# Last inverse DFT stage on quarter tiles of the array, and gated sums clamped at -1 in place of a Relu pass

## The chip, the core and the metric

One core of a Trainium2 chip runs the whole kernel as one program. The metric is the device time of one execution in microseconds, the median of several runs. What the trace shows is one further execution, with a profiler on.

## The reference

The input `x` is 8 x 3072 x 256 in float32. Along the 3072 positions each batch is transformed, mixed with a complex 256 x 256 weight, shrunk towards zero and transformed back; then a two-layer network with a gate runs over all 24576 rows.

```python
X = np.fft.rfft(x, axis=1)
Yr = Xr @ w_r - Xi @ w_i + b_r
Yi = Xr @ w_i + Xi @ w_r + b_i
Yr = np.sign(Yr) * np.maximum(np.abs(Yr) - lam, 0.0)     # lam = 0.01, the same for Yi
y = np.fft.irfft(Y, n=x.shape[1], axis=1)
h = y.reshape(B * S, D) @ w_in                           # 256 -> 2048
g = np.where(h >= 1, h, np.where(h <= -1, 0.0, (h + 1) ** 2 / 4))
out = g @ w_out                                          # 2048 -> 256
```

## The kernel before

The transform of length 3072 = 48 x 64 is done by matmuls. The first part of the program (up to about 566 us) runs a loop over 96 units `u` (8 batches x 12 pairs of frequency groups): `stage1` and `stage2` are the forward transform, `mix` multiplies with the complex weights, `shrink` shrinks, `stage3` is the first half of the inverse transform and stores its result to DRAM (`u_d`).

The last inverse stage is `stage4`. Its unit is a block `c` of four positions: `load_u(c)` brings 96 rows x 4 positions x 256 channels from `u_d` to `uin`; 64 blocks cover everything. For each half of 128 channels (`d`) and each position (`jj`) one float32 matmul takes 96 rows x 128 channels of `uin` as the stationary operand and the 96 x 96 table `c2_sb` as the moving one. In the trace every float32 matmul stands as two passes, each with a weight load (LDWEIGHTS on the row PEld) and a MATMUL: 8 matmuls of a block are 16 of each. `stage4_out` copies a half-block of results (128 x 384) from PSUM to `yt`, on ScalarE. The table `c2` couples a row 2g+c, which holds one of two parities `h`, only with columns of the same parity, so half of its entries are zero.

The second part is the network, a loop over 384 units `n`: 48 tiles of 512 rows, each with 8 pairs of 128 hidden columns. Each pair is formed by seven products of half-size blocks (Strassen's scheme in Winograd's form, `product`, three matmuls each, since every factor is split in a high and a low part), in PSUM tiles `ps_yz` (tag C) and `ps_xv` (tag D). `snap` copies a partial sum to SBUF (ScalarE), `sum_first` and `sum_second` add on VectorE to give `h`; then `ramp` (Relu of 0.5 h + 0.5) and `square` on ScalarE, `gate` on VectorE (max with 1, min with the square), `split_hi` (ScalarE) and `split_lo` (VectorE), and three units later `down` multiplies with `w_out` into the accumulators `accA` and `accB`, in eight pieces `D_(0..7)` that stand between the products. The program is written out by hand in this order; each engine runs its own instructions in the order in which they are issued, and waits on semaphores for the others.

`stage4` of the first two half-batches (8 blocks) lies in the last units of the first part and in units 0 and 1 of the second (`quarter4`, `leftover`). The other 56 blocks lie one each at the end of 56 of the 384 units of the second part, behind `D_(4, 5, 6, 7)` (`if n in four`), in two buffers of tag D.

Of the kernel before, what the change touches and what calls it, by code (L numbers as in the profile page):

```python
# [8 lines left out]

F32 = mybir.dt.float32  # L10
# [11 lines left out]
LAM = 0.01  # L22


def dft_constants(S):
# [55 lines left out]
    return np.stack([hi, round_r(a - hi.astype(np.float64))])  # L81


def constants(S):
    c1, c2, t, ti = dft_constants(S)
    return {
        "c1": np.ascontiguousarray(parts(c1).transpose(1, 0, 2)),
        "c2": c2.astype(np.float32),
        "t": np.ascontiguousarray(t.transpose(1, 0, 2).astype(np.float32)),
        "ti": np.ascontiguousarray(ti.transpose(1, 0, 2).astype(np.float32)),  # L90
    }
# [3 lines left out]
def tile_fft_mix_moe(  # L95
    ctx: ExitStack, tc: tile.TileContext, x, w_r, w_i, b_r, b_i, w_in, w_out, c1, c2, t_f, t_i, out
):
    nc = tc.nc
    B, S, D = x.shape
    DFF = w_in.shape[1]  # L100
    NF = DFF // P
    ND = D // P
    JT = 4
# [12 lines left out]
    NUNIT = NT * NP  # L116

    left = lambda name, **k: tc.alloc_tile_pool(name=name, bufs=1, side="left", reuse_waits="tile", **k)
# [15 lines left out]
    ug = [a.rearrange("(g p) j d -> (p j) g d", g=G) for a in u_d]  # L134


    win = [[keep.tile([P, 7, P], F32R, name=f"win{k}{p}") for p in range(NP)] for k in "hl"]
    wout = keep.tile([P, NF, 2, D], F32R, name="wout")
    c2_sb = keep.tile([Q, Q], F32, name="c2_sb")
    half = keep.tile([P, 1], F32, name="half")  # L140

    c1_sb = first_st.tile([Q, 2, Q], F32R, name="c1_sb")
# [4 lines left out]
    bias = fold.tile([P, D], F32, name="bias")  # L147
# [255 lines left out]
    def stage4(c, d, into=None):  # L403
        hb, m = divmod(c, JH // JT)
        a = uin[c] if d < ND - 1 else uin.pop(c)
        if m == 0 and d == 0:
            yt[hb] = pools["in"].tile([P, ND, Q, JH], F32, tag="yt", bufs=2, name="yt")
        if into is None:
            bufs_D = 2 if "ff" in pools else 3
            ps = pools["ps"].tile([P, JT, Q], F32, tag="D", bufs=bufs_D, name="ps_i2")  # L410
        else:
            ps = into.rearrange("p k d -> p (k d)")[:, : JT * Q].rearrange("p (j q) -> p j q", j=JT)
        ps4[c, d] = ps
        for jj in range(JT):
            nc.tensor.matmul(ps[:, jj, :], lhsT=a[:, jj, d * P : (d + 1) * P], rhs=c2_sb, start=True, stop=True)  # L415
        if d == ND - 1 and c + 3 < NHB * JH // JT:
            load_u(c + 3)

    def stage4_out(c, d, copy=nc.scalar.copy):
        hb, m = divmod(c, JH // JT)  # L420
        copy(yt[hb][:, d, :, m * JT : (m + 1) * JT], ps4.pop((c, d)).rearrange("p j q -> p q j"))

    ops, raw_t = {}, {}

# [36 lines left out]
    ups, snaps, hs, rs, gs, acc, outs = {}, {}, {}, {}, {}, {}, {}  # L463
# [5 lines left out]
    def product(n, which, to, start):  # L469

        i, p = divmod(n, NP)
        if n not in ups:
            ups[n] = [
                pools["ps"].tile([P, 2, TH], F32, tag="C", bufs=2, name="ps_yz"),
                pools["ps"].tile([P, 2, TH], F32, tag="D", bufs=2, name="ps_xv"),
            ]
        ps = ups[n]["YZXV".index(to) // 2][:, "YZXV".index(to) % 2, :]
        w, m = FACTORS[which - 1]
        hi, lo = ops[i]
        for k, (a, mv) in enumerate(((0, hi), (0, lo), (1, hi))):  # L480
            nc.tensor.matmul(  # L481
                ps, lhsT=win[a][p][:, w, :], rhs=mv[:, m, :], start=start and k == 0, stop=k == 2, skip_group_check=True
            )


    def snap(n, at):
        if n not in snaps:
            snaps[n] = pools["ff"].tile([P, 3, TH], F32, tag="snap", bufs=2, name="snap")
        nc.scalar.copy(snaps[n][:, at, :], ups[n][1][:, 0, :])  # L489


    def sum_second(n):
        h = hs[n] = pools["ff"].tile([P, 4, TH], F32, tag="h", bufs=3, name="h")
        yz, xv = ups[n]
        for to, a in ((2, yz[:, 0, :]), (3, xv[:, 1, :])):
            nc.vector.tensor_tensor(out=h[:, to, :], in0=a, in1=snaps[n][:, 2, :], op=ALU.add)

    def sum_first(n):
        yz, xv = ups.pop(n)
        nc.vector.tensor_tensor(out=hs[n][:, 0:2, :], in0=yz, in1=snaps.pop(n)[:, 0:2, :], op=ALU.add)  # L500

    ALL = slice(0, 4)

    def ramp(n, part=ALL):
        if n not in rs:
            rs[n] = pools["ff"].tile([P, 4, TH], F32, tag="r", bufs=2, name="r")
        nc.scalar.activation(rs[n][:, part], hs[n][:, part], AF.Relu, bias=half, scale=0.5)  # L507

    def square(n, part=ALL):
        nc.scalar.activation(rs[n][:, part], rs[n][:, part], AF.Square)  # L510

    def gate(n, part=ALL):
        h, r = hs[n][:, part], rs[n][:, part]
# [11 lines left out]
    def down(n, piece):  # L525
        if n < 0 or n >= NUNIT:
            return
# [63 lines left out]
    with tc.manual_schedule():  # L591
# [21 lines left out]
        for h in range(FIRST):  # L613
            last = xs[h][0]
# [37 lines left out]
            next(ws, None)  # L652

        stored = FIRST
        four = iter([(c, d) for c in range(2 * JH // JT) for d in range(ND)])

        def quarter4():
            c, d = next(four)
            stage4(c, d)
            stage4_out(c, d)  # L660

        U4 = UN - 6

# [3 lines left out]
        for u in range(UN + 3):  # L667
# [51 lines left out]
            if 1 <= u < UN + 1:  # L719
                shrink(u - 1, more_weights if WU <= u < 84 else lambda: None)  # L720
            if U4 <= u < U4 + 4:
                quarter4()
                quarter4()
            if u == U4 + 4:
                prep_sums(0)
            if u == UN:
                mixing.release()
                pools["ops"] = right("ops")
                prep_split_hi(0, 0)
                prep_split_hi(0, 1)  # L730
                prep_split_lo(0, 0)
                quarter4()
            if u == UN + 1:
                quarter4()
                quarter4()
            if 2 <= u < UN + 2:
                stage3(u - 2)
            if u == UN + 1:
                prep_split_hi(0, 2)
                quarter4()  # L740
                prep_split_lo(0, 1)
                prep_split_lo(0, 2)
        fold.release()
# [3 lines left out]

        LAG = 3
        spare = [pools["ps"].tile([P, 2, 2, D], F32, tag=k, bufs=1, name=f"spare{k}") for k in "AB"]
        rest = [(c, d, spare[k // 2][:, k % 2]) for k, (c, d) in enumerate(four)]  # L750
        four = {}

        def leftover(n):
            if n < NP and rest:
                c, d, into = rest.pop(0)
                stage4(c, d, into)
                stage4_out(c, d, nc.vector.tensor_copy)

        for hb in range(2, NHB):
            for m, at in enumerate((0, 7, 11, 16)):  # L760
# [2 lines left out]
        for n in range(NUNIT + LAG + 1):  # L763
            i, p = divmod(n, NP)
            live = n < NUNIT
            split_step = p - 4 if live and i + 1 < NT and 4 <= p < 7 else None
            n1 = n - 1 if 0 <= n - 1 < NUNIT else None
            n2 = n - 2 if 0 <= n - 2 < NUNIT - 1 else None
            last = n1 == NUNIT - 1
# [9 lines left out]
            if live:  # L779
                product(n, 1, "X", True)  # L780
                snap(n, 1)
                if n == 0:
                    leftover(n)
                product(n, 5, "Y", True)
                if n == 0:
                    leftover(n)
                product(n, 2, "Z", False)
            if out_b is not None:
                output_copy(out_b, 1)
# [7 lines left out]
            if n1 is not None:  # L797
                product(n1, 3, "Y", False)
                sum_first(n1)
            if n == 1:  # L800
                leftover(n)
            if live:
                product(n, 6, "X", False)
                snap(n, 0)
# [7 lines left out]
                output_copy(out_a, 0)  # L812
                output_add(out_a, 0)
            if n1 is not None and not last:
                ramp(n1)
            if last:
                for part in (slice(2, 4), slice(0, 2)):
                    ramp(n1, part)
                    square(n1, part)
                    gate(n1, part)  # L820
                    split_hi(n1, part)
                    split_lo(n1, part)
            if live:
                product(n, 4, "V", False)
                if n == 0:
                    leftover(n)
# [40 lines left out]
```

## Time and profile before

| what | value |
|---|---|
| median of 3 runs | 2732.16 us (2730.28 to 2732.48) |
| the profiled execution | 2729.93 us |
| its span, first to last instruction | 2728.1 us |
| mean granted clock of TensorE | 0.998 of full speed |
| PE busy, share of the span | 2703.3 us, 99% |
| VectorE busy | 2106.2 us, 77% |
| ScalarE busy | 2068.1 us, 76% |
| GpSimd busy | 379.2 us, 14% |

PE stands for TensorE's matmuls, PEld for its weight loads, which overlap the matmuls; DVE is VectorE, ACT is ScalarE, POOL is GpSimd. The span is 1.8 us shorter than the time of its execution. PE's busy time counts every matmul's modelled duration, so two that overlap in the pipeline cover the same time once, and a share of 99% says that PE is nearly never without one, not that it works at its peak.

### The profile page before, as it was taken

The numbers are of one execution on the slowest core, as the hardware profiler recorded it, in microseconds if no ns is written. First come the engines' busy times: TensorE is split into PE (matmuls) and PEld (weight loads), VectorE is DVE, ScalarE is ACT, GpSimd is POOL, SyncE is SP. The second block draws the span as 40 slices with busy tenths as digits, with TensorE's granted clock in tenths as the row PEclk, the third lists the DMA queues.
The fourth block names the chain that finished last, engine by engine and source line by source line (L and its number), as shares of the span: only waits on it lengthen the run. The fifth ranks groups of instructions, "written<-read, shape, count | busy, mean of one in ns | idle before, by whom it ended". The sixth has DMA issues, their size and how long they took to land.

```text
span 2728.1 us, 48377 instructions
## 1 busy us (share of the span) xinstructions
PE 2703.3 (99%) x19296; PEld 2520.5 (92%) x19296; DVE 2106.2 (77%) x2987; ACT 2068.1 (76%) x3458; POOL 379.2 (14%) x372
## 2 busy tenths in 40 slices
PE   8999999999999999999999999999999999999998
PEld 5999999989999999999999999999999999999997
DVE  5899988668777777777777777777777777777786
ACT  5677777567777777787877777777777777777786
POOL 1255433010101010101010010101010101010100
PEclk9999999999999999999999999999999999999999
DMA  8766666410000001000000000000001010100000
GB/s 252 229 215 215 213 215 198 140 58 16 20 28 20 28 20 28 20 28 20 28 20 28 23 25 24 24 28 21 28 20 30 18 34 14 34 14 22 9 17 16
DMA packets 123548, 166.57 MB, mean 61 GB/s; under 512 B 10842, under 2 KB 88506, under 8 KB 123322
## 3 DMA queue, kind: packets, MB, share of 16 engines
q1 hardware_dynamic: 123074, 163.26, 19.8%
q8 instruction: 152, 2.49, 0.4%
q14 instruction: 74, 0.61, 0.1%
q10 hardware_dynamic: 248, 0.20, 0.0%
HBM read 87.93 MB, written 75.50 MB: 60 GB/s over the span
## 4 chain that ended last, share of the span: by engine, by line
PE 95%; DVE 2%; ACT 2%; DMA 1%; issue 0%; SPq 0%; ACTq 0%
PE ps_xv L481 20%; PE ps_yz L481 15%; PE accB L537 13%; PE accA L537 13%; PE ps_mix L260 9%; PE accB L540 7%; PE accA L540 7%; PE ps_i L415 4%; PE ps_f L192 3%; PE ps_f L213 3%; PE ps_i L297 2%; DVE yl L288 0%; DVE xl L180 0%; ACT xh L175 0%; DVE Xl L230 0%
## 5 line engine op out<-in xcount | busy, mean ns | idle before, releaser
L489 ACT COPY snap<-ps_xv 128x256 f32<-128x256 f32 x1152 | 425.6, 369 | 415.4 <-PE ps_xv L481 415.4
L523 DVE TENSOR_TENSOR gl<-h,gh 128x1024 fp32r<-128x1024 f32 x385 | 470.4, 1222 | 258.2 <-ACT gh L519 251.8
L537 PE MATMUL accA<-wout,gh 128*128 128x512 f32 x1536 | 574.3, 396 | 0.6 <-ACT gh L519 0.6
L537 PE MATMUL accB<-wout,gh 128*128 128x512 f32 x1536 | 558.0, 396 | 0.0
L514 DVE SCALAR_TENSOR_TENSOR h<-h,r 128x1024 f32<-128x1024 f32 x385 | 475.3, 1235 | 78.4 <-ACT r L510 78.3
L507 ACT ACTIVATE r<-h,half 128x1024 f32<-128x1024 f32 x385 | 443.8, 1153 | 0.0
L481 PE MATMUL ps_xv<-oph,winh 128*128 128x256 f32 x1536 | 437.6, 285 | 1.7 <-ACT snap L489 1.4
L481 PE MATMUL ps_xv<-opl,winh 128*128 128x256 f32 x1536 | 437.2, 285 | 0.0
L481 PE MATMUL ps_xv<-oph,winl 128*128 128x256 f32 x1536 | 432.0, 281 | 0.0
L540 PE MATMUL accB<-wout,gl 128*128 128x256 f32 x1536 | 429.7, 280 | 0.0
L540 PE MATMUL accA<-wout,gl 128*128 128x256 f32 x1536 | 428.7, 279 | 1.0 <-DVE gl L523 1.0
L510 ACT ACTIVATE r<-r 128x1024 f32<-128x1024 f32 x385 | 410.2, 1066 | 0.1
L519 ACT CAST gh<-h 128x1024 fp32r<-128x1024 f32 x385 | 404.6, 1051 | 2.9 <-DVE h L514 2.9
L500 DVE TENSOR_TENSOR h<-ps_yz,snap 128x512 f32<-128x512 f32 x384 | 265.2, 691 | 132.9 <-PE ps_yz L481 106.5
L436 POOL TENSOR_TENSOR tsum<-yt 128x256 f32<-128x256 f32 x96 | 100.6, 1062 | 1916.4 <-DVE opl L457 1098.6
L537 PEld LDWEIGHTS accB<-wout,gh 128*128 128x128 f32 x1536 | 288.0, 188 | 52.7
L481 PE MATMUL ps_yz<-oph,winl 128*128 128x256 f32 x1152 | 325.4, 282 | 0.0
L481 PE MATMUL ps_yz<-opl,winh 128*128 128x256 f32 x1152 | 324.8, 282 | 0.0
L481 PE MATMUL ps_yz<-oph,winh 128*128 128x256 f32 x1152 | 322.0, 280 | 0.1
L537 PEld LDWEIGHTS accA<-wout,gh 128*128 128x128 f32 x1536 | 288.0, 188 | 36.3 <-ACT gh L519 0.9
L481 PEld LDWEIGHTS ps_xv<-oph,winh 128*128 128x128 f32 x1536 | 288.2, 188 | 34.7 <-ACT snap L489 2.7
L481 PEld LDWEIGHTS ps_xv<-oph,winl 128*128 128x128 f32 x1536 | 292.3, 190 | 0.0
(114 smaller groups left out, 5437.5 us busy)
## 6 DMA issues: line engine op xcount, KB each, us to landing
xin<-in_x SPq DMA_DIRECT2D x128, 192.0 KB
z_d<-zst SPq DMA_DIRECT2D x128, 192.0 KB
zin<-z_d SPq DMA_DIRECT2D x96, 256.0 KB
u_d<-ust SPq DMA_DIRECT2D x96, 256.0 KB
uin<-u_d SPq DMA_DIRECT2D x64, 384.0 KB
out<-ot SPq DMA_DIRECT2D x191, 128.0 KB
wraw<-in_moe_w_in SPq DMA_DIRECT2D x16, 256.0 KB
wraw<-in_moe_w_out SPq DMA_DIRECT2D x16, 256.0 KB
```

The costliest lines, as they stand in the source:

```text
L260: nc.tensor.matmul(ps[:, gi, :], lhsT=a, rhs=wm[nm, k][:, d, :], start=n == 0, stop=n == 6 * ND - 1)
L415: nc.tensor.matmul(ps[:, jj, :], lhsT=a[:, jj, d * P : (d + 1) * P], rhs=c2_sb, start=True, stop=True)
L481: nc.tensor.matmul(ps, lhsT=win[a][p][:, w, :], rhs=mv[:, m, :], start=start and k == 0, stop=k == 2, skip_group_check=True)
L489: nc.scalar.copy(snaps[n][:, at, :], ups[n][1][:, 0, :])
L500: nc.vector.tensor_tensor(out=hs[n][:, 0:2, :], in0=yz, in1=snaps.pop(n)[:, 0:2, :], op=ALU.add)
L507: nc.scalar.activation(rs[n][:, part], hs[n][:, part], AF.Relu, bias=half, scale=0.5)
L510: nc.scalar.activation(rs[n][:, part], rs[n][:, part], AF.Square)
L514: nc.vector.scalar_tensor_tensor(out=h, in0=h, scalar=1.0, in1=r, op0=ALU.max, op1=ALU.min)
L519: nc.scalar.copy(gs[n][0][:, part], hs[n][:, part])
L523: nc.vector.tensor_tensor(out=gl, in0=hs[n][:, part], in1=gh.bitcast(F32), op=ALU.subtract)
L537: nc.tensor.matmul(o, lhsT=gh[:, blk, at : at + P], rhs=wout[:, f], start=f == 0, stop=False, skip_group_check=True)
L540: nc.tensor.matmul(o[:, 0, :], lhsT=gl[:, blk, at : at + P], rhs=wout[:, f, 0, :], start=False, stop=f == NF - 1, skip_group_check=True,)
```

## The change

Three things are changed together.

`stage4` uses the array in quarters. The 96 rows of a block are stored in two sets of 48 rows, one per parity, at partitions 0 and 64 (`load_u` issues two DMAs per block, each of half the bytes), and `c2_sb` holds the 48 x 48 table of either parity, without the zero entries. For each position and each half of 128 channels there are now four float32 matmuls, each with 48 rows x 64 channels as the stationary operand and 48 columns of moving data, on the four 64 x 64 quarters of the array (`tile_position`), in the order (row set, channel half) = (0,0), (1,1), (0,1), (1,0). Both halves `d` of a block are done in one call; each row set writes a PSUM bank of its own, and two copies of 384 elements, one for each bank, take the result to `yt`.

In the second part `stage4` stands ahead of `sum_second` and `D_(4, 5, 6, 7)` in its unit instead of at its end, and its two banks are one of tag D and the C bank that is not the unit's own (C is now two tags, C0 and C1, used in turn).

The sums `h` are clamped from below at -1 as they are formed (`add_floor`, a custom VectorE operation that adds and limits), so that (0.5 h + 0.5) is never negative; the Relu pass `ramp` is gone, and `square` reads `h` with scale and bias itself, at the place at which `ramp` stood.

```diff
-        uin[c] = pools["in"].tile([Q, JT, D], F32, tag="uin", bufs=3, name="uin")
+        uin[c] = pools["in"].tile([P, JT, D], F32, tag="uin", bufs=3, name="uin")
         j = half_b * JH + m * JT
-        nc.sync.dma_start(uin[c], u_d[b][:, j : j + JT, :])
+        for h in range(2):
+            nc.sync.dma_start(uin[c][h * HP : h * HP + R1], uh[b][h, :, j : j + JT, :])
...
         for jj in range(JT):
-            nc.tensor.matmul(ps[:, jj, :], lhsT=a[:, jj, d * P : (d + 1) * P], rhs=c2_sb, start=True, stop=True)
+            for d in range(ND):
+                for h, e in QUARTERS:
+                    rows, cols = slice(h * HP, h * HP + R1), slice(e * HP, (e + 1) * HP)
+                    nc.tensor.matmul(
+                        ps[h][cols, d, jj, :],
+                        lhsT=a[rows, jj, d * P + e * HP : d * P + (e + 1) * HP],
+                        rhs=c2_sb[rows],
+                        start=True,
+                        stop=True,
+                        tile_position=(h * HP, e * HP),
+                    )
...
+    def add_floor(out, a, b):
+        nc.vector._custom_dve(TENSOR_ADD_SAT, out=out, in0=a, in1=b, s0=FLT_MAX, s1=-1.0)
...
-    def ramp(n, part=ALL):
+    def square(n, part=ALL):
         if n not in rs:
             rs[n] = pools["ff"].tile([P, 4, TH], F32, tag="r", bufs=2, name="r")
-        nc.scalar.activation(rs[n][:, part], hs[n][:, part], AF.Relu, bias=half, scale=0.5)
-
-    def square(n, part=ALL):
-        nc.scalar.activation(rs[n][:, part], rs[n][:, part], AF.Square)
+        nc.scalar.activation(rs[n][:, part], hs[n][:, part], AF.Square, bias=half, scale=0.5)
...
                 product(n, 7, "X", False)
                 snap(n, 2)
+                if n in four:
+                    stage4(four[n], [bank("D", 2), bank(f"C{(n + 1) % 2}")])
+                    stage4_out(four[n], [nc.scalar.copy] * 2)
                 sum_second(n)
-            if n1 is not None and not last:
-                square(n1)
             D_(4, 5, 6, 7)
...
-            if n in four:
-                for d in range(ND):
-                    stage4(four[n], d)
-                    stage4_out(four[n], d)
```

On PE, at the end of a unit of the second part with a block, the rows before were these (`accB<-wout` is a piece of `down`, `ps_i` is `stage4`, `ps_xv` with `winh` and `oph` a product of the next unit; the semaphores of an engine carry its name):

```order
L537 MATMUL accB<-wout,gh 128x512
L540 MATMUL accB<-wout,gl 128x256
L415 MATMUL ps_i_24909<-c_sb,uin 128x96 [waits DMAHW4_49,DVE_49]
L415 MATMUL ps_i_24909<-c_sb,uin 128x96 x3
L415 MATMUL ps_i_24915<-c_sb,uin 128x96 [waits DVE_49,Activation_49]
L415 MATMUL ps_i_24915<-c_sb,uin 128x96 x3
```

In the changed kernel the block begins directly behind the unit's last product, and the first rows of its 32 are these, which go on by turns between the two banks:

```order
L505 MATMUL ps_xv<-oph,winh_91 128x256
L505 MATMUL ps_xv<-opl,winh_91 128x256
L505 MATMUL ps_xv<-oph,winl_99 128x256
L429 MATMUL ps_i_25574<-c_sb,uin 64x48 [waits DMAHW1_49,DVE_49]
L429 MATMUL ps_i_25575<-c_sb,uin 64x48 [waits DMAHW2_49,DVE_49]
```

So 8 matmuls of 128 x 96 behind the pieces of `down` have become 32 of 64 x 48 ahead of them.

On ACT the same kind of unit had these rows before (`gh` is `split_hi`, `r<-h` is `ramp`, `r<-r` is `square`, `yt` is `stage4_out`):

```order
L519 CAST gh<-h 128x1024 [waits DVE_49]
L507 ACTIVATE r<-h,half 128x1024 [waits DVE_49]
L489 COPY snap<-ps_xv 128x256 [waits PE_49]
L510 ACTIVATE r<-r 128x1024 [waits Activation_49]
L421 COPY yt<-ps_i_11571 128x96x4 [waits PE_49]
L421 COPY yt<-ps_i_11577 128x96x4 [waits PE_49]
```

Now there is one pass over `h` instead of two:

```order
L543 CAST gh<-h 128x1024 [waits DVE_49]
L534 ACTIVATE r<-h,half 128x1024 [waits DVE_49]
L513 COPY snap<-ps_xv 128x256 [waits PE_49]
L444 COPY yt<-ps_i_11849 128x96x4 [waits PE_49]
L444 COPY yt<-ps_i_11850 128x96x4 [waits PE_49]
```

The row `r<-r` is gone, and the two copies of the block follow the snap directly.

## Rows read from the trace of the kernel before

**Rows 1.** The page's head: span, busy time and share of each engine.

```profile
span 2728.1 us, 48377 instructions
PE 2703.3 (99%) x19296; PEld 2520.5 (92%) x19296; DVE 2106.2 (77%) x2987; ACT 2068.1 (76%) x3458; POOL 379.2 (14%) x372
```

**Rows 2.** The page's chain that ended last, shares by line.

```profile
PE ps_xv L481 20%; PE ps_yz L481 15%; PE accB L537 13%; PE accA L537 13%; PE ps_mix L260 9%; PE accB L540 7%; PE accA L540 7%; PE ps_i L415 4%; PE ps_f L192 3%; PE ps_f L213 3%; PE ps_i L297 2%; DVE yl L288 0%; DVE xl L180 0%; ACT xh L175 0%; DVE Xl L230 0%
```

**Rows 3.** Windows, from:to, length, then each engine's busy time (instructions), clock, DMA.

```profile
566.00:590.00 24.00, 21.19 (x153) 18.82 (x152) 14.25 (x22) 14.43 (x25) 2.83 (x4) 1.00 0.29 78
...
650.00:1200.00 550.00, 550.00 (x3884) 514.40 (x3883) 419.65 (x550) 430.92 (x681) 50.69 (x49) 1.00 0.08 24
```

**Rows 4.** The chain in order of time: start us, us, what.

```profile
519.94 0.72 PE ps_i L297 x6
...
524.43 0.72 PE ps_i L297 x6
525.15 0.89 PE ps_f L213 x8
...
530.67 0.75 PE ps_i L297 x6
...
692.95 0.72 PE ps_xv L481 x6
698.27 0.72 PE ps_xv L481 x6
...
705.38 0.72 PE ps_xv L481 x6
```

**Rows 5.** Timeline of PE and PEld at one block: start us, us, what.

```profile
700.12 1.87 PEld L415 LDWEIGHTS ps_i<-c_sb,uin 96*128 96x128 f32 x16
700.23 1.92 PE L415 MATMUL ps_i<-c_sb,uin 96*128 96x96 f32 x16
...
701.91 0.19 PEld L481 LDWEIGHTS ps_xv<-oph,winh 128*128 128x128 f32 x1
701.94 0.36 PE L481 MATMUL ps_xv<-oph,winh 128*128 128x256 f32 x1
702.02 0.19 PEld L481 LDWEIGHTS ps_xv<-opl,winh 128*128 128x128 f32 x1
```

**Rows 6.** Weight loads by form: count, busy us, mean ns, idle us before.

```profile
L415 PEld LDWEIGHTS ps_i<-c_sb,uin 96*128 96x128 f32 x992 | 116.2, 192 | 2.6
...
L192 PEld LDWEIGHTS ps_f<-xh,c_sb 96*96 96x96 f32 x208 | 30.4, 163 | 3.4
```

**Rows 7.** ACT's groups by form in the second part.

```profile
L507 ACT ACTIVATE r<-h,half 128x1024 f32<-128x1024 f32 x383 | 442.3, 1155 | 0.0
...
L489 ACT COPY snap<-ps_xv 128x256 f32<-128x256 f32 x1152 | 425.6, 369 | 415.4 <-PE ps_xv L481 415.4
L510 ACT ACTIVATE r<-r 128x1024 f32<-128x1024 f32 x383 | 409.0, 1068 | 0.0
L519 ACT CAST gh<-h 128x1024 fp32r<-128x1024 f32 x383 | 403.3, 1053 | 1.3 <-DVE h L514 1.3
...
L421 ACT COPY yt<-ps_i 128x384 f32<-128x384 f32 x124 | 59.5, 480 | 58.5 <-PE ps_i L415 58.5
```

**Rows 8.** DVE's groups by form in the second part.

```profile
L514 DVE SCALAR_TENSOR_TENSOR h<-h,r 128x1024 f32<-128x1024 f32 x383 | 474.0, 1237 | 77.7 <-ACT r L510 77.7
L523 DVE TENSOR_TENSOR gl<-h,gh 128x1024 fp32r<-128x1024 f32 x383 | 469.0, 1225 | 256.8 <-ACT gh L519 250.3
...
L500 DVE TENSOR_TENSOR h<-ps_yz,snap 128x512 f32<-128x512 f32 x384 | 265.2, 691 | 132.9 <-PE ps_yz L481 106.5
...
L496 DVE TENSOR_TENSOR h<-ps_yz,snap 128x256 f32<-128x256 f32 x384 | 163.1, 425 | 30.1 <-ACT snap L489 1.9
```

**Rows 9.** The chain in order of time at the program's end.

```profile
2713.17 0.63 ACT r L507
...
2715.88 0.63 ACT r L507
```

More of the change, by code (lines that the diff above doesn't have):

```diff
@@ L8 @@
 from concourse._compat import with_exitstack
+from concourse.dve_ops import TENSOR_ADD_SAT
 F32 = mybir.dt.float32
@@ L22 @@
 LAM = 0.01
+FLT_MAX = float(np.finfo(np.float32).max)
 def dft_constants(S):
@@ L81, in parts, with two_rows @@
     return np.stack([hi, round_r(a - hi.astype(np.float64))])
+def two_rows(a):
+    o = np.zeros((P, a.shape[1]), a.dtype)
+    for h in range(2):
+        o[h * P // 2 : h * P // 2 + len(a)] = a
+    return o
 def constants(S):
@@ L87, in constants @@
         "c1": np.ascontiguousarray(parts(c1).transpose(1, 0, 2)),
-        "c2": c2.astype(np.float32),
+        "c2": two_rows(c2.reshape(R1, 2, R1, 2)[:, 0, :, 0].astype(np.float32)),
         "t": np.ascontiguousarray(t.transpose(1, 0, 2).astype(np.float32)),
@@ L116, in tile_fft_mix_moe @@
     NUNIT = NT * NP
+    HP = P // 2
+    QUARTERS = ((0, 0), (1, 1), (0, 1), (1, 0))
     left = lambda name, **k: tc.alloc_tile_pool(name=name, bufs=1, side="left", reuse_waits="tile", **k)
@@ L134, in tile_fft_mix_moe @@
     ug = [a.rearrange("(g p) j d -> (p j) g d", g=G) for a in u_d]
+    uh = [a.rearrange("(r h) j d -> h r j d", h=2) for a in u_d]
     win = [[keep.tile([P, 7, P], F32R, name=f"win{k}{p}") for p in range(NP)] for k in "hl"]
     wout = keep.tile([P, NF, 2, D], F32R, name="wout")
-    c2_sb = keep.tile([Q, Q], F32, name="c2_sb")
+    c2_sb = keep.tile([P, R1], F32, name="c2_sb")
     half = keep.tile([P, 1], F32, name="half")
@@ L398, in load_u, with stage4 @@
         b, half_b = divmod(hb, 2)
-        uin[c] = pools["in"].tile([Q, JT, D], F32, tag="uin", bufs=3, name="uin")
+        uin[c] = pools["in"].tile([P, JT, D], F32, tag="uin", bufs=3, name="uin")
         j = half_b * JH + m * JT
-        nc.sync.dma_start(uin[c], u_d[b][:, j : j + JT, :])
-    def stage4(c, d, into=None):
+        for h in range(2):
+            nc.sync.dma_start(uin[c][h * HP : h * HP + R1], uh[b][h, :, j : j + JT, :])
+    def stage4(c, banks):
         hb, m = divmod(c, JH // JT)
-        a = uin[c] if d < ND - 1 else uin.pop(c)
-        if m == 0 and d == 0:
+        a = uin.pop(c)
+        if m == 0:
@@ L416, in stage4 @@
-        if d == ND - 1 and c + 3 < NHB * JH // JT:
+        ps = ps4[c] = [
+            x.rearrange("p a n -> p (a n)")[:, : ND * JT * R1].rearrange("p (d j r) -> p d j r", d=ND, j=JT)
+            for x in banks
+        ]
+        for jj in range(JT):
+            for d in range(ND):
[9 more added lines that the diff above has]
+                    )
@@ L417, in stage4, with stage4_out @@
+        if c + 3 < NHB * JH // JT:
             load_u(c + 3)
-    def stage4_out(c, d, copy=nc.scalar.copy):
+    def stage4_out(c, copies):
         hb, m = divmod(c, JH // JT)
-        copy(yt[hb][:, d, :, m * JT : (m + 1) * JT], ps4.pop((c, d)).rearrange("p j q -> p q j"))
+        to = yt[hb][:, :, :, m * JT : (m + 1) * JT].rearrange("p d (r h) j -> p d r h j", h=2)
+        for h, (copy, ps) in enumerate(zip(copies, ps4.pop(c), strict=True)):
+            copy(to[:, :, :, h, :], ps.rearrange("p d j r -> p d r j"))
@@ L425, in tile_fft_mix_moe, with bank @@
+    def bank(tag, bufs=1):
+        return pools["ps"].tile([P, 2, TH], F32, tag=tag, bufs=bufs, name="ps_i2")
     ops, raw_t = {}, {}
@@ L473, in product @@
             ups[n] = [
-                pools["ps"].tile([P, 2, TH], F32, tag="C", bufs=2, name="ps_yz"),
+                pools["ps"].tile([P, 2, TH], F32, tag=f"C{n % 2}", bufs=1, name="ps_yz"),
                 pools["ps"].tile([P, 2, TH], F32, tag="D", bufs=2, name="ps_xv"),
@@ L495, in sum_second @@
         for to, a in ((2, yz[:, 0, :]), (3, xv[:, 1, :])):
-            nc.vector.tensor_tensor(out=h[:, to, :], in0=a, in1=snaps[n][:, 2, :], op=ALU.add)
+            add_floor(h[:, to, :], a, snaps[n][:, 2, :])
     def sum_first(n):
         yz, xv = ups.pop(n)
-        nc.vector.tensor_tensor(out=hs[n][:, 0:2, :], in0=yz, in1=snaps.pop(n)[:, 0:2, :], op=ALU.add)
+        add_floor(hs[n][:, 0:2, :], yz, snaps.pop(n)[:, 0:2, :])
     ALL = slice(0, 4)
-    def ramp(n, part=ALL):
+    def square(n, part=ALL):
         if n not in rs:
             rs[n] = pools["ff"].tile([P, 4, TH], F32, tag="r", bufs=2, name="r")
-        nc.scalar.activation(rs[n][:, part], hs[n][:, part], AF.Relu, bias=half, scale=0.5)
-    def square(n, part=ALL):
-        nc.scalar.activation(rs[n][:, part], rs[n][:, part], AF.Square)
+        nc.scalar.activation(rs[n][:, part], hs[n][:, part], AF.Square, bias=half, scale=0.5)
     def gate(n, part=ALL):
@@ L654, in tile_fft_mix_moe, with half4 @@
         stored = FIRST
[L655 to L660, printed above, removed]
+        four = iter(range(2 * JH // JT))
+        def half4():
+            c = next(four)
+            stage4(c, [bank(k) for k in "AB"])
+            stage4_out(c, [nc.scalar.copy] * 2)
         U4 = UN - 6
@@ L721, in tile_fft_mix_moe @@
             if U4 <= u < U4 + 4:
-                quarter4()
-                quarter4()
+                half4()
             if u == U4 + 4:
@@ L731, in tile_fft_mix_moe @@
                 prep_split_lo(0, 0)
-                quarter4()
+                half4()
             if u == UN + 1:
-                quarter4()
-                quarter4()
+                half4()
             if 2 <= u < UN + 2:
@@ L749, in tile_fft_mix_moe, with leftover @@
         spare = [pools["ps"].tile([P, 2, 2, D], F32, tag=k, bufs=1, name=f"spare{k}") for k in "AB"]
-        rest = [(c, d, spare[k // 2][:, k % 2]) for k, (c, d) in enumerate(four)]
+        rest = [(c, [x[:, k] for k in range(2)]) for c, x in zip(four, spare, strict=True)]
         four = {}
[L753 to L757, printed above, removed]
+        def leftover():
+            c, banks = rest.pop(0)
+            stage4(c, banks)
+            stage4_out(c, [nc.vector.tensor_copy] * 2)
         for hb in range(2, NHB):
@@ L781, in tile_fft_mix_moe @@
                 snap(n, 1)
-                if n == 0:
-                    leftover(n)
                 product(n, 5, "Y", True)
                 if n == 0:
-                    leftover(n)
+                    leftover()
                 product(n, 2, "Z", False)
@@ L814, in tile_fft_mix_moe @@
             if n1 is not None and not last:
-                ramp(n1)
+                square(n1)
             if last:
                 for part in (slice(2, 4), slice(0, 2)):
-                    ramp(n1, part)
                     square(n1, part)
```

11 lines of the change are left out of this document (1 added, 10 removed).

## The prediction

> **What bounds the kernel now.** I read the page's head first: PE is busy for 2703.3 us of 2728.1, VectorE and ScalarE for about three quarters [rows 1]. The chain that ended last is PE nearly all the way, and `stage4` (L415) has 4% of it [rows 2]. Busy PE can hide waits, so I then took windows: in the 550 us from 650 to 1200 PE has no idle time at all, while ACT works 430.92 and DVE 419.65 us; only the change of stages, 566 to 590, shows PE idle, 24.00 - 21.19 = 2.8 us [rows 3]. What the second part costs is therefore what PE's instructions cost in a row. The chain in order of time gives the price of a block of `stage4` twice: a unit of the second part takes 698.27 - 692.95 = 5.32 us, the one with a block 705.38 - 698.27 = 7.11, so 1.79 us; a unit of the first part takes 524.43 - 519.94 = 4.49, with a block 530.67 - 524.43 = 6.24, so 1.75 [rows 4]. The timeline agrees: the 16 weight loads of a block begin at 700.12 and the next product's load at 701.91, 1.79 us or 112 ns for each load with its pass [rows 5]. 64 blocks are 64 x 1.79 = 115 us; this is all that the first edit can touch.
>
> **What limits a block.** The passes of `stage2` stream 128 float32 columns and take 0.89 / 8 = 111 ns [rows 4], those of `stage4` stream 96 and take 112. Fewer columns do not make a pass shorter, so it is the load of 128 stationary columns that sets the pace, not the stream. Halving the moving columns alone would then gain nothing; what counts is the loads, now 64 of half the width per block in place of 16. A load of 96 columns lasts 163 ns, one of 128 192 [rows 6]: 29 / 32 = 0.9 ns per column. A load of 64 columns should thus pace at 112 - 58 = 54 ns, by proportion at 56; I take 55 (estimate). A stream of 48 columns takes at most 111 x 48 / 128 = 42 ns (estimate).
>
> **The first edit, from both sides.** No row of before shows a quarter of the array at work, so the price of a block hangs on how many quarters load at once:
> - one at a time: 64 x 55 ns = 3.52 us, 1.73 more than now;
> - two at a time, one per row set: 1.76 us, nothing gained;
> - all four: 0.88 us, 0.91 less.
>
> In between lies the case that I take. The two passes of one call use the same quarter, so the second follows the first by a stream (42 ns); the next call is on other rows, and its load can have run meanwhile. Then a block costs 32 x 42 ns = 1.34 us. What speaks for hidden loads is that now already a load begins while the pass before it streams (load at 702.02, matmul from 701.94 to 702.30, on the same rows) [rows 5], and that the order (0,0), (1,1), (0,1), (1,0) never has the same row set twice in succession.
>
> Going into quarters and back has no row either. Below it costs nothing; above, a whole load and a whole pass are exposed at each end, 2 x (0.19 + 0.36) = 1.1 us by the load and the matmul of the next product [rows 5]. I take 0.11 us, one pass, nearer to the lower end, since loads run ahead under other work in these rows. So 1.45 us for 1.79, a gain of 0.34; 64 x 0.34 = 21.8 us.
>
> The Trainium skill, TensorE: Matmul & The Clock Gate, section Part 3: Packing small matmuls, says that weight loads overlap running matmuls only where the row group differs, and that matmuls start strictly in program order. The trace disagrees on the first for the undivided array, where the load at 702.02 starts under a matmul on the same 128 rows; for quarters no run here shows it. By the rule the second pass of a call would wait for the first and then load, and the sum would be that of rival 4.
>
> **The second edit, Relu.** 383 Relu passes of 1155 ns go; the Square that remains reads `h` with scale and bias, and I price it like the Relu that did so, 1155 for 1068 [rows 7]. ACT then needs per unit 3 x 0.37 + 1.16 + 1.05 = 3.32 us where it needed 4.38, of 5.32. That is relief for an engine that PE does not wait for, so in the middle of the second part it is worth nothing: PE covers it. It counts where ACT is on the chain. At the end two Relu pieces of 0.63 us stand in it [rows 9]: 1.3 us. At the change of stages PE is idle for 2.8 us [rows 3], of which I give 1.2 to the shorter chain. Together 2.5 us; bounds 1.3 and 4.1.
>
> **The third, the sums.** The clamped add is one VectorE pass with two inputs, as before. The pass with two operations (L514) takes 1237 ns for 1024 elements, 1.21 per element, the plain add 691 for 512, 1.35 [rows 8]: a further operation per element costs nothing in these rows, so I price the edit at zero. DVE uses 0.69 + 2 x 0.42 + 1.24 + 1.23 = 4.0 of 5.32 us per unit. Were an add to cost twice as much, 1.53 us more would make 5.5, and DVE would be the bound.
>
> **What moves.** The block stands before `D_(4..7)` now, which are the `accB` matmuls: 13% + 7% of 2728 us over 384 units [rows 2], 1.4 us each. This hides two things. The next unit's first product writes the D bank of this unit, so it must wait for `sum_second`; and its Y product writes the C bank of the block, so it waits for ACT's second copy. ACT needs 2 x 0.48 us [rows 7] after the block plus the snap ahead of them, less than the 1.4 us and the first product's 0.36. If that cover were gone, a copy of 0.48 us would come onto PE's path in each of 56 units, 27 us. The block itself now waits for the previous unit's readers of both banks, which ran a unit earlier. Behind its first wait stand only PE's own rows. SP issues two loads of half the bytes per block for one of all, still three blocks ahead, where the DMA engines are busy 8% [rows 3]; should one come late, PE would stand for it in full.
>
> **Sum.** 2729.9 - 21.8 - 2.5 = 2705.6 us for the profiled execution; the median of the runs before is 2.2 us above their profiled one, so 2708 us, 0.9% faster.
>
> **Rivals.**
> 1. All four quarters load side by side. Price 0.88 + 0.11 = 0.99 us, 64 x 0.80 = 51 us, 2679 us. For it: the quarters share no cell, and no two neighbours in the order share their rows. Against it: 128 instructions in 0.99 us are 8 ns each, where the shortest spacing of passes in these rows is 111 ns [rows 4].
> 2. Two at a time, and the changeover costs more than a pass. 1.76 us of loads and 0.1 to 1.1 us for going in and out: 0.07 to 1.07 us more per block, that is 2734 to 2798; with 0.4 us of changeover, towards the lower end, 64 x 0.37 - 2.5 = 21 us more, 2753. It decides for slower once a block costs over 1.9 us. For it: the two passes of a call need the same quarter's weights one after another, 32 x 55 ns, if a load can only begin when the pass before has begun. This is also the case in which the edit gains nothing: with no changeover it ends within 0.2% of before. The Trainium skill, TensorEngine Tiling (Array Packing), section Key Properties, says that a change of tiling mode drains the array; no run here shows what that costs.
> 3. The clamped add takes a second pass: DVE bounds the units at 5.5 us, 384 x 0.2 = 77 us and more, 2790 or above.
> 4. The quarters do not overlap at all. Loads alone 3.52 us; if in a quarter each load waits for the pass before it, 32 x (55 + 42) = 3.1. With 0.11, 1.42 to 1.84 more per block: 2821 to 2848. For it: every pass in these rows waits for its own load.
>
> **How the numbers follow.** A measurement of this kernel tells about 0.2% (5.5 us) from no change. Chances: forecast 0.40; rival 1 0.17; rival 2 0.25, of it 0.08 within 0.2%; rival 3 0.03; rival 4 0.15. A block of 1.75 instead of 1.45 would put the forecast itself within 0.2%, which takes 0.02 from it. So faster 0.55, same 0.10, slower 0.35. The range leaves out rivals 3 and 4 and a little at the low end, where four quarters load and the changeover is free, and reaches over the rest: 2677 to 2798. The forecast's own range, a block at 1.2 to 1.7 us, is 2692 to 2724.
>
> **What the profile would show.** Right: units with a block 6.7 to 6.8 us apart, 64 loads of about 130 ns duration per block, starting 15 to 30 ns apart; no PE wait on ACT or DVE in the second part; ACT busy down by about 410 us, DVE unchanged; sums still at 691 and 425 ns. Wrong: passes 55 ns apart (rivals 2 and 4), a gap at either end of a block over 0.2 us (rival 2), sums above 1 us (rival 3), units with a block longer than 7.11 us.

## The result, and the profile after

The changed kernel takes 2698.28 us (median of 4 runs, 2696.92 to 2699.14) against 2731.22 for the kernel before (four runs; the table ahead of the prediction has the first three); the ratio is 0.9879, with a 95% interval of 0.9862 to 0.9896. That is 1.2% faster, where 0.9% was forecast (2708 us).

The head of the page after, to be held against [rows 1]: PE still fills 99% of a span that is 32.4 us shorter, and ACT has fallen from 76% to 64%.

```profile
span 2695.7 us, 54265 instructions
PE 2670.8 (99%) x22368; PEld 2481.0 (92%) x22368; DVE 2078.7 (77%) x2987; ACT 1715.8 (64%) x3073; POOL 385.0 (14%) x372
```

The chain in order of time (start us, us, what) gives the price of a block as in [rows 4]. A unit of the first part takes 523.63 - 519.15 = 4.48 us, one with a block 534.95 - 529.20 = 5.75: a block costs 1.27 for 1.75. In the second part a unit takes 5.31 and one with a block 704.70 - 698.11 = 6.59: 1.28 for 1.79.

```profile
519.15 0.72 PE ps_i L309 x6
523.63 0.72 PE ps_i L309 x6
...
529.20 0.91 PE ps_i L309 x6
...
534.95 0.91 PE ps_i L309 x6
...
692.80 0.72 PE ps_xv L505 x6
698.11 0.72 PE ps_xv L505 x6
...
704.70 0.72 PE ps_xv L505 x6
```

The timeline at the same block, as in [rows 5]:

```profile
698.55 0.28 PE L505 MATMUL ps_xv<-oph,winl 128*128 128x256 f32 x1
698.76 1.02 PEld L429 LDWEIGHTS ps_i<-c_sb,uin 48*64 48x64 f32 x64
698.76 1.15 PE L429 MATMUL ps_i<-c_sb,uin 48*64 48x48 f32 x64
...
699.84 0.19 PEld L561 LDWEIGHTS accB<-wout,gh 128*128 128x128 f32 x1
699.84 0.50 PE L561 MATMUL accB<-wout,gh 128*128 128x512 f32 x1
```

The reader should see three things. 64 loads and 64 passes, four times as many as before, start within 0.93 us. The first load starts at 698.76, 0.21 us after the matmul before it started, where loads of undivided products start right behind the matmul before them. And the first load after the block does not run ahead either: it starts at 699.84 together with its own matmul, which then lasts 0.50 us. The starts of the passes (the MATMUL rows) in this block lie as follows (differences in ns, the first 16 behind the first round of four):

```
6 7 7 38 | 7 6 7 38 | 7 7 6 39 | 6 7 7 38
```

That is rounds of four passes, one every 58 ns, 6 to 7 ns apart within a round: four quarters at work at once.

Groups by form, against [rows 6 to 8]: the load of 64 columns lasts 134 ns, the Square that reads `h` with a bias 1153 ns (priced at 1155), the clamped add 690 for 691.

```profile
L534 ACT ACTIVATE r<-h,half 128x1024 f32<-128x1024 f32 x383 | 441.8, 1153 | 0.0
...
L517 DVE CUSTOM_DVE_ANT_0 h<-ps_yz,snap 128x512 f32<-128x512 f32 x384 | 264.9, 690 | 195.5 <-PE ps_yz L505 195.5
...
L429 PEld LDWEIGHTS ps_i<-c_sb,uin 48*64 48x64 f32 x3968 | 63.6, 134 | 8.6
```

At the change of stages, however, something was lost. The windows (columns as in [rows 3]: PE, PEld, DVE, ACT, POOL, then granted clock, DMA share, GB/s) show PE busy for 0.60 of 2.00 us, and after that a clock granted at half, the lower of the two levels, 1.2 GHz:

```profile
564.00:566.00 2.00, 0.60 (x3) 0.20 (x2) 0.54 (x1) 1.70 (x3) 0.00 (x0) 1.00 0.91 234
...
568.00:572.00 4.00, 3.54 (x64) 3.15 (x57) 1.02 (x2) 0.37 (x1) 1.59 (x3) 0.50 0.41 97
...
576.00:578.00 2.00, 1.85 (x12) 1.64 (x11) 0.98 (x3) 0.47 (x2) 0.00 (x0) 0.78 0.41 125
```

What PE waited for there, from 560 to 590 (us in total, times, longest): the second and third of these lines are new. Two waits of the kernel before, 0.8 us of the first leftover half-block for ACT's copy `yt` and 0.3 of the second for DVE's, are gone, so that the sum of the waits went from 2.5 to 3.8 us (with 0.2 for DVE's `yl`, not shown).

```profile
PE ps_xv L505 <- ACT snap L513: 1.4, 3, 0.5
PE ps_yz L505 <- ACT oph L477: 1.3, 1, 1.3
PE ps_yz L505 <- DVE opl L481: 0.9, 1, 0.9
```

Where the 32.4 us of the span came from, by landmarks that both chains have. In the kernel before they are the end of the last `stage3`, the first unit at full pace and the last unit:

```profile
565.47 0.92 PE ps_i L297 x6
...
586.55 0.72 PE ps_xv L481 x6
...
2705.37 0.71 PE ps_yz L481 x6
```

In the changed kernel:

```profile
563.12 0.75 PE ps_i L309 x4
...
586.53 0.72 PE ps_xv L505 x6
...
2674.07 0.72 PE ps_yz L505 x6
```


| stretch | before | after | difference |
|---|---|---|---|
| first part, to the end of the last `stage3` | 566.39 | 563.87 | -2.5 |
| change of stages, to the first unit that runs at full pace | 20.16 | 22.66 | +2.5 |
| second part, to the last unit | 2118.82 | 2087.54 | -31.3 |
| end | 22.73 | 21.63 | -1.1 |

56 blocks at 1.79 - 1.28 = 0.51 us are 28.6 of the 31.3; the other 2.7 are the units themselves, 5.313 us for 5.320 (experiment 9). The first row is less sure than the others: with the same first part, the last `stage3` ends at 562.39 us in the trace of experiment 7 and at 565.17 in that of experiment 1. Six blocks at 0.48 us make 2.9.

### The profile page after: what moved, and what is told of

Same layout as the page of the kernel before. It is cut to its first block, busy times and chain, and to the rows that moved or that the text cites. A ratio compares the mean times of both kernels' runs of the same rounds, so it can differ in the third digit from the quotient of the medians.

```text
span 2695.7 us, 54265 instructions
## 1 busy us (share of the span) xinstructions
PE 2670.8 (99%) x22368; PEld 2481.0 (92%) x22368; DVE 2078.7 (77%) x2987; ACT 1715.8 (64%) x3073; POOL 385.0 (14%) x372
## 4 chain that ended last, share of the span: by engine, by line
PE 94%; DVE 3%; ACT 2%; DMA 1%; issue 0%; SPq 0%; ACTq 0%
PE ps_xv L505 20%; PE ps_yz L505 15%; PE accB L561 14%; PE accA L561 13%; PE ps_mix L272 8%; PE accB L564 7%; PE accA L564 7%; PE ps_f L204 3%; PE ps_f L225 3%; PE ps_i L429 2%; PE ps_i L309 2%; DVE yl L300 1%; ACT xh L187 0%; DVE xl L192 0%; DVE Xl L242 0%
## 5 line engine op out<-in xcount | busy, mean ns | idle before, releaser
L517 DVE CUSTOM_DVE_ANT_0 h<-ps_yz,snap 128x256 f32<-128x256 f32 (+1 forms) x768 | 427.8, 557 | 224.1 <-PE ps_yz L505 195.5
L460 POOL TENSOR_TENSOR tsum<-yt 128x256 f32<-128x256 f32 x96 | 106.6, 1130 | 1879.5 <-DVE opl L481 1090.1
L564 PEld LDWEIGHTS accA<-wout,gl 128*128 128x128 f32 x1536 | 288.8, 188 | 1.8 <-DVE gl L547 1.8
```

Of the source, the lines that this page charges most:

```text
L460: nc.gpsimd.tensor_tensor(out=t[:, to], in0=a, in1=b, op=ALU.subtract)
L517: nc.vector._custom_dve(TENSOR_ADD_SAT, out=out, in0=a, in1=b, s0=FLT_MAX, s1=-1.0)
L564: nc.tensor.matmul(o[:, 0, :], lhsT=gl[:, blk, at : at + P], rhs=wout[:, f, 0, :], start=False, stop=f == NF - 1, skip_group_check=True,)
```

## The experiments

Theory: a block costs 16 rounds of four loads that run side by side (0.93 us) and 0.35 us for taking the array into quarters and back; ScalarE is not waited for. Rivals: the order of the calls makes it possible; the lighter ScalarE carries part; the shorter stream does. Medians of the kernel before, taken beside each group of runs, were 2729.83 (experiments 1 to 4), 2732.28 (5 to 8) and 2729.68 (9, 10).

**1. Quarters, but Relu kept.**

```diff
-            add_floor(h[:, to, :], a, snaps[n][:, 2, :])
+            nc.vector.tensor_tensor(out=h[:, to, :], in0=a, in1=snaps[n][:, 2, :], op=ALU.add)
...
-                square(n1)
+                ramp(n1)
...
                 sum_second(n)
+            if n1 is not None and not last:
+                square(n1)
```

> The quarters and the moved block alone; sums are added without the clamp, and Relu and Square stay two passes. Theory (TensorE's instructions set the time, and a block of the last stage fell from 1.79 to 1.28 us): 56 blocks x 0.51 = 28.6 us and 2.9 from the six blocks of the first part stay, only the 1.1 us of the end and what the shorter ScalarE chain gives at the change of stages are lost: 2699 to 2702 us. Rival (the lighter ScalarE carries part of the gain, by copies that come in time): units with a block show PE waiting for ACT, and the time is 2706 us or more. The units without a block tell a third thing: they went from 5.320 to 5.313 us, 2.6 us over 384; if that is the Relu's doing they go back to 5.320.

Measured: 2699.83 us, ratio 0.9884 (0.9869 to 0.9899). The chain in order of time:

```profile
695.46 0.72 PE ps_xv L505 x6
700.77 0.72 PE ps_xv L505 x6
...
707.36 0.72 PE ps_xv L505 x6
```

Units are 5.31 us and the block 6.59 - 5.31 = 1.28, as in the changed kernel: the second part owes nothing to the Relu's going. The end takes 22.7 us again.

**2. Relu removed and sums clamped, last inverse stage as before.**

```diff
-            nc.vector.tensor_tensor(out=h[:, to, :], in0=a, in1=snaps[n][:, 2, :], op=ALU.add)
+            add_floor(h[:, to, :], a, snaps[n][:, 2, :])
...
             if n1 is not None and not last:
-                ramp(n1)
+                square(n1)
...
                 sum_second(n)
-            if n1 is not None and not last:
-                square(n1)
             D_(4, 5, 6, 7)
```

> The clamp and the missing Relu pass alone; the last inverse stage is as before. Theory: ScalarE is not what TensorE waits for, so only the end (1.1 us) and the change of stages (0 to 1.2 us) gain: 2728.5 to 2730 us against 2731, perhaps not to be told from before. If the units of 5.313 us come from the Relu, another 2.6 us: 2726. Rival (ScalarE's relief is worth its share): 10 us or more.

Measured: 2729.03 us, ratio 0.9994 (0.9985 to 1.0003), not to be told from before. The end shrank to 21.7 us, as in the changed kernel; the units did not move:

```profile
693.30 0.72 PE ps_xv L483 x6
698.62 0.72 PE ps_xv L483 x6
```

The change of stages, from the end of the last `stage3` to the first unit at full pace, takes 586.90 - 567.43 = 19.47 us for 20.16:

```profile
566.52 0.91 PE ps_i L299 x6
...
586.90 0.72 PE ps_xv L483 x6
```

So a ScalarE pass of 1.1 us per unit, 442 us in all, is worth 1.0 us at the end and 0.7 at the change of stages in these traces, and nothing between them.

**3. Row sets alone: 48 rows, 128 channels per load.**

```diff
-                for h, e in QUARTERS:
+                for h in range(2):
...
-                        lhsT=a[rows, jj, d * P + e * HP : d * P + (e + 1) * HP],
+                        lhsT=a[rows, jj, d * P : (d + 1) * P],
...
-                        tile_position=(h * HP, e * HP),
+                        tile_position=(h * HP, 0),
```

> Two row sets of 48 rows, but all 128 channels in one load: 16 calls per block, 32 loads of 128 columns, two of them on different rows. Theory (a load takes a time by its columns, and loads of different tiles run side by side): 16 rounds of 112 ns = 1.79 us, plus 0.35 for going in and out, 2.14 per block; 64 x 0.86 = 55 us above the changed kernel, 2753 us. Rival (the stream or the zero entries set the price, so half the columns give the gain): a block as cheap as now or cheaper, 1.0 to 1.28 us, 2680 to 2698 us.

Measured: 2752.48 us, ratio 1.0081 (1.0067 to 1.0094), slower than before.

```profile
706.11 0.72 PE ps_xv L505 x6
...
713.53 0.72 PE ps_xv L505 x6
```

The block costs 7.42 - 5.31 = 2.11 us. The streams are as short as in the changed kernel and the zero entries are gone too, so neither is the gain; with loads of 128 columns, two side by side, a round takes 112 ns as before (in the trace the passes of a block start 7 and 105 ns apart by turns).

**4. Quarter by quarter: all eight calls of one quarter, then the next.**

```diff
-        for jj in range(JT):
-            for d in range(ND):
-                for h, e in QUARTERS:
+        for h, e in QUARTERS:
+            for jj in range(JT):
+                for d in range(ND):
```

> The same 32 calls of a block, but all eight of one quarter before the next quarter's. Theory (matmuls start in program order, and each pass waits for its own quarter's load of 58 ns): nothing can overlap, 64 x 58 ns = 3.7 us + 0.35, 4.1 per block; 64 x 2.8 = 180 us more, 2877 us. Rival (the engine picks out of its queue whatever quarter is free): as the changed kernel, 2698 us; in between if it looks ahead some calls only.

Measured: 2857.64 us, ratio 1.0465 (1.0451 to 1.048).

```profile
716.66 0.72 PE ps_xv L505 x6
...
725.44 0.72 PE ps_xv L505 x6
```

The block costs 8.78 - 5.31 = 3.47 us, between the theory's 4.1 and the rival's 1.28. The starts of the passes at a border of two quarters (ns apart) show why:

```
... 58 58 59 | 6 52 41 17 41 18 41 | 58 58 59 ...
```

Within one quarter passes come 58 ns apart, but about four of them run beside the first four of the next quarter: the engine takes passes of another quarter ahead of their turn, a few, not all. The rows do not name the quarter; this is inferred from the spacing, since eight passes start within 216 ns where those of one quarter take 58 each. The blocks make 64 x (3.47 - 1.28) = 140 of the 159 us above the changed kernel; in the rest is a clock that fell to its lower level more often (last section).

**5. Neighbouring calls on the same rows.**

```diff
-    QUARTERS = ((0, 0), (1, 1), (0, 1), (1, 0))
+    QUARTERS = ((0, 0), (0, 1), (1, 0), (1, 1))
```

> The order of the four quarters is (0,0), (0,1), (1,0), (1,1): neighbours share their rows. Theory (all four quarters load at once, whatever the order): 2698 us, rounds of four still 58 ns apart. Rival (a load only hides under a pass on other rows): two quarters of one row set follow one another, 16 x 2 x 58 ns = 1.87 us + 0.35 per block, 64 x 0.94 = 60 us more, 2758 us.

Measured: 2696.70 us, ratio 0.9869 (0.9855 to 0.9882).

```profile
696.99 0.72 PE ps_xv L505 x6
...
703.58 0.72 PE ps_xv L505 x6
```

The block is 6.59 - 5.31 = 1.28 again: alternating the row sets buys nothing.

**6. Each block in two parts, two of the four remaining `down` pieces between.**

```diff
...
-                    stage4(four[n], [bank("D", 2), bank(f"C{(n + 1) % 2}")])
-                    stage4_out(four[n], [nc.scalar.copy] * 2)
+                    stage4(four[n], [bank("D", 2), bank(f"C{(n + 1) % 2}")], range(2))
                 sum_second(n)
-            D_(4, 5, 6, 7)
+            D_(4, 5)
+            if n in four:
+                stage4(four[n], None, range(2, 4))
+                stage4_out(four[n], [nc.scalar.copy] * 2)
+            D_(6, 7)
```

> In the second part each of the 56 blocks is cut in two, with half of the four pieces of the down product between them, so that the array goes into quarters and back twice per block. Theory (going in and out costs 0.35 us beside 0.93 for the rounds): 56 x 0.35 = 19 us more, 2717 us. Rival (the 0.35 us is no changeover but belongs to the matmuls themselves, or the first loads hide): 2698 to 2702 us.

Measured: 2716.94 us, ratio 0.9941 (0.9928 to 0.9955).

```profile
697.84 0.72 PE ps_xv L507 x6
698.56 0.61 PE ps_i L429 x32
...
700.07 0.61 PE ps_i L429 x32
...
704.78 0.72 PE ps_xv L507 x6
```

The unit with a block takes 6.94 for 6.59 us: one more way into quarters and back costs 0.35 us, as read off the block itself.

**7. Both leftover blocks ahead of the first Y product of unit 0.**

```diff
                 snap(n, 1)
+                if n == 0:
+                    leftover()
+                    leftover()
                 product(n, 5, "Y", True)
-                if n == 0:
-                    leftover()
                 product(n, 2, "Z", False)
...
                 product(n, 4, "V", False)
-                if n == 0:
-                    leftover()
```

> Both leftover blocks of the first half-batches stand ahead of the first Y product of unit 0, on TensorE where it now waits 1.27 us for ScalarE and 0.88 for VectorE. Theory (the two waits make the clock fall to its lower level for 10 us, and the blocks there and the products take longer): the waits are covered, the clock stays at the upper level, 3 to 4 us less, 2694 to 2695 us. Rival (the clock falls for the drop in work at the change of stages as such, or the blocks' data come too late): the clock falls all the same, 2697 to 2699 us.

Measured: 2691.38 us (2689.43 to 2691.66), ratio 0.9848 (0.9834 to 0.9861), the best version of this study: 5.3 us under experiment 5, which ran beside it, and 6.9 under the changed kernel. The windows show the clock at the upper level throughout:

```profile
564.00:568.00 4.00, 3.54 (x98) 3.27 (x90) 3.07 (x5) 0.64 (x3) 2.63 (x4) 1.00 0.87 249
568.00:574.00 6.00, 5.07 (x39) 4.56 (x38) 3.74 (x7) 3.63 (x8) 0.21 (x1) 1.00 0.24 44
```

In PE's waits from 560 to 590 those for `oph` and `opl` are gone:

```profile
PE ps_xv L505 <- ACT snap L513: 1.4, 3, 0.5
PE spareA L429 <- ACT ust L313: 0.3, 1, 0.3
```

The gain is larger than the 3 to 4 us expected. The change of stages takes 578.54 - 562.39 = 16.15 us for the changed kernel's 22.66, 6.5 less:

```profile
561.64 0.75 PE ps_i L309 x4
...
578.54 0.72 PE ps_xv L505 x6
```

An estimate from the two traces: about 1.9 us are waits (3.8 in the changed kernel, 1.9 here, from 560 to 590); about 1.8 are the two blocks (2.0 us for both together, where each took 1.89); and most of the rest are the products, which start 0.21 us apart at the lower level and 0.12 at the upper.

**8. Channel halves alone: 96 rows, 64 channels per load, the dense table.**

```diff
...
-                for h, e in QUARTERS:
-                    rows, cols = slice(h * HP, h * HP + R1), slice(e * HP, (e + 1) * HP)
+                for e in range(2):
                     nc.tensor.matmul(
-                        ps[h][cols, d, jj, :],
-                        lhsT=a[rows, jj, d * P + e * HP : d * P + (e + 1) * HP],
-                        rhs=c2_sb[rows],
+                        ps[d][e * HP : (e + 1) * HP, jj, :],
+                        lhsT=a[:, jj, d * P + e * HP : d * P + (e + 1) * HP],
+                        rhs=c2_sb,
...
-                        tile_position=(h * HP, e * HP),
+                        tile_position=(0, e * HP),
```

> Two halves of 64 channels, but 96 rows in one set with the dense 96 x 96 table: 16 calls per block, 32 loads of 64 columns, two side by side, and streams of 96 columns. Theory: a round of two takes the longer of a load (58 ns) and a stream of 96 float32 columns (at most 83 ns, estimate from 111 ns at 128): 16 x 83 = 1.33 us + 0.35 = 1.68 per block, 64 x 0.40 = 26 us above the changed kernel, 2724 us; if the load sets the round, 1.28 and 2698 us. Rival (loads on the same rows cannot run side by side): 32 x 58 = 1.87 + 0.35, 2758 us.

Measured: 2723.18 us, ratio 0.9966 (0.9954 to 0.9978).

```profile
699.48 0.71 PE ps_xv L503 x6
...
706.48 0.71 PE ps_xv L503 x6
```

The block costs 7.00 - 5.32 = 1.68 us, what the theory gave: two loads on the same 96 rows do run side by side, and now the round has the 83 ns estimated for the stream of 96 columns, where a load takes 58 (in the trace the passes start 7 and 76 ns apart by turns).

**9. The small table padded to its former size.**

```diff
-    c2_sb = keep.tile([P, R1], F32, name="c2_sb")
+    c2_sb = keep.tile([P, 2 * R1], F32, name="c2_sb")[:, :R1]
```

> The changed kernel with 192 bytes more per partition reserved for the small table, so that what is allocated behind it lies at the addresses of before; nothing else differs. Units without a block took 5.320 us in every kernel with the table of 96 columns (before, Relu removed only, channel halves only) and 5.313 in every one with the table of 48. Theory (the 7 ns come from where the operands lie in SBUF): 5.320 again, 384 x 0.007 = 2.6 us more than the changed kernel, 2700 to 2701 us. Rival (they come from the two row sets or the split C buffers, which the kernel with channel halves shares only in part): 5.313 and 2697 to 2698 us.

Measured: 2699.16 us, ratio 0.9884 (0.9867 to 0.99). The medians do not settle 2.6 us; the chain does, since the units went back to 5.32:

```profile
587.19 0.72 PE ps_xv L505 x6
592.51 0.72 PE ps_xv L505 x6
```

**10. Two calls of a quarter in succession.**

```diff
-            for d in range(ND):
-                for h, e in QUARTERS:
+            for h, e in QUARTERS:
+                for d in range(ND):
```

> The order of a block's 32 calls is by pairs: both channel halves d of one quarter, then the next quarter, so four passes in succession are on one quarter. Quarter by quarter, passes came 58 ns apart in one quarter, and some four passes of a quarter ran beside the first four of the next. Theory (each quarter takes its passes from a short lookahead of about four passes): the other quarters still find work, and a block costs 1.28 to 1.5 us, 2698 to 2712 us. Rival (calls start in strict program order, and only a call's own two passes run by themselves): of each pair the second call must wait for the first, 16 x 2 x 58 ns = 1.87 + 0.35 = 2.2 us per block, 64 x 0.94 = 60 us more, 2758 us.

Measured: 2702.10 us, ratio 0.9896 (0.9881 to 0.9911).

```profile
698.21 0.72 PE ps_xv L505 x6
...
704.88 0.72 PE ps_xv L505 x6
```

The block costs 6.67 - 5.31 = 1.36 us, near to 1.28 and far from the 2.2 of strict program order. The lookahead of experiment 4 is enough for four passes in succession on one quarter.

## Why the prediction was right, and where its steps were off

- **The bound.** PE's instructions in a row set the time, and a block's 1.79 us is all that could be touched: right. In the second part after the first units, PE waits 0.7 us in all (from 590 to 2690 us), near the end.
- **Loads set the pace, not streams.** Right, and shown by experiments 3 and 8. The load of 64 columns was estimated at 55 ns; the round takes 58. The stream of 96 columns, estimated at 83 at most, gave the block of experiment 8 to within the reading.
- **How many quarters load at once.** This step failed: the prediction took 32 x 42 ns = 1.34 us, the second pass of a call holding up the next call. All four quarters load side by side, 16 x 58 = 0.93 us, the case that stood as rival 1 with 0.17. Experiments 4 and 10 show what takes the place of the assumption: a quarter's passes are 58 ns apart, but the engine starts passes of the other quarters meanwhile, as far as the spacing of the starts tells. The order of the row sets, named there as speaking for hidden loads, does not matter (experiment 5). The Trainium skill, TensorE: Matmul & The Clock Gate, section Part 3: Packing small matmuls, says in its list of what overlaps that loads overlap running matmuls only where the row group differs, and that matmuls start in program order. This case's traces agree with neither: neighbours on the same rows leave a block at 1.28 us (experiment 5) and two halves on the same 96 rows cost 1.68 where loads one after another would need 2.2 (experiment 8); two calls of a quarter in succession cost 1.36 where program order would need 2.2 (experiment 10).
- **The changeover.** Also mis-sized, the other way: 0.11 us taken, within bounds of 0 and 1.1; it is 0.35 (block 1.28 - 0.93, and experiment 6). In experiment 7 the two leftover blocks stand directly behind each other, and their 128 passes start within 1.86 us, 32 rounds of 58 ns: a block that follows another in quarters pays nothing for the way in. By the two errors, -0.41 and +0.24, a block came out at 1.28 instead of 1.45. That the forecast lies only 10 us from the measured time is partly luck: with the loads put right and the changeover left at 0.11 it would have been 1.04 us for a block and 2682 us, further off on the other side. The Trainium skill, TensorEngine Tiling (Array Packing), section Key Properties, says that a change of tiling mode drains the array. The timeline is in line with it: the first load starts 0.21 us behind the start of the matmul before it, and the first load after the block starts at 699.84 with its own matmul.
- **Relu.** Worth nothing in the middle: right (experiments 1 and 2). At the end 1.1 us against 1.3 predicted. Of the 1.2 us granted at the change of stages experiment 2 shows 0.7, with the clock at its upper level there; in the changed kernel the next point hides it, and the stretch became 2.5 us longer.
- **The change of stages.** Not foreseen. A half-block that stood between the last `stage3` and the first product went ahead of that `stage3`, and the leftover block moved behind the first Y product, so nothing stood between the first product and a product whose operands ACT and DVE were still splitting; PE waited 1.3 and 0.9 us, the clock fell to its lower level for about 10 us, and both leftover blocks ran there in 1.9 us instead of 1.1. Experiment 7 puts them ahead and removes the waits, the fall and more than the loss. How long the lower level lasts is not set by these waits alone: behind nearly the same ones it lasted 3 us in experiment 10 and 14 in experiment 1, so 1 or 2 us between the traces of such runs need not come from their edits.
- **The clamped add.** Priced at zero: right, 690 for 691 ns.
- **The cover of the move.** Right: the block's copies and `sum_second` lie under the `accB` pieces, and no unit with a block in the chain shows a wait. No run left the quarters at the end of the unit, so what the move itself is worth is not shown.

## What to carry to other kernels

When a matmul's rows or columns leave part of the array idle, ask first whether loads or streams set its pace: here narrower loads on four quarters gave the gain, and shorter streams alone (experiment 3) gave a loss. Count the ways into tiled mode and back, and keep calls of different tiles close to each other in the order. When PE's work shrinks at a change of stages, look at what the removed work had covered: two waits of 2.2 us together were followed there by about 10 us at the lower clock.

## What the hardware showed that had not been expected

- Quarters start passes 6 to 7 ns apart and, by the spacing of the starts, out of program order within a short lookahead: about four passes at a border in experiment 4.
- 192 bytes more per partition in front of the other buffers make every unit of the second part 5.320 instead of 5.313 us (experiment 9). All kernels with the small table had 5.313, all with the large one 5.320. That the shift of the addresses does it is shown; which operand it is stays open.
- In experiment 4 the clock fell to its lower level ten times in the second part, 34 us in all, although PE had work without a break. Each time a block, with its narrow passes nearly all one at a time, had ended less than 1 us before; but there are 56 such blocks, and what else it takes was not tried. One of the ten (columns as in [rows 3]):

```profile
925.00:930.00 5.00, 5.00 (x61) 4.62 (x58) 1.89 (x3) 0.96 (x3) 0.00 (x0) 0.78 0.38 107
930.00:931.00 1.00, 1.00 (x7) 1.00 (x7) 0.00 (x0) 0.38 (x2) 0.00 (x0) 0.50 0.01 0
```
